# Loading the first two batches' q and k per head pair in runs of six tokens, and starting attention first, in a fused attention and multiplicative-FFN kernel

## The chip, the cores and the metric

The kernel runs on one core of a Trainium2 chip. The metric is the device time of one execution in microseconds (us), as the median of several runs. The record marks a run as ordinary or slow. PE is TensorE, DVE VectorE, ACT ScalarE, POOL GpSimd. "Span" is the length of the profiled execution, some 2 us shorter than the device time.

## The reference

Attention over 8 batches and 8 heads, 576 tokens of width 64, with 16 unmasked "beacon" keys and values in front of each sequence, then a feed-forward part without a nonlinearity, whose last two matrices are one product:

```python
scores = scale * np.matmul(q, concat([beacon_k, k]).T)       # causal over the tokens, beacons visible to all
a = exp(scores - max); a /= a.sum(-1)
attn = np.matmul(a, concat([beacon_v, v]))                   # [B=8, H=8, S=576, D=64]
x = attn.transpose(0, 2, 1, 3).reshape(4608, 512)
out = ((x @ w1) * (x @ w2) @ w3) @ w_out                     # w1, w2 512x1024, w3 1024x1024, w_out 1024x512
```

## The kernel before

All matmuls are fp16. Scores are made transposed, so each batch needs q and k as qT, kT: a head pair's 128 dimensions on the partitions, tokens in order along the free axis. From batch 2 on a DMA transposes them (30 transfers into qT and 30 into kT in the trace, 7.3 and 7.5 us in the median from issue to landing). Batches 0 and 1 are transposed on PE from token tiles of all heads, loaded through POOL's queue, which casts fp32 to fp16 on the way (the trace counts 128 KB for a tile of 128x512, two bytes a value):

```python
def load_q(b, c):                        # load_k, load_v alike; runs of 64 fp32 values per token and head
    nc.gpsimd.dma_start(
        q16s[b % NB2][:rows, c, :].rearrange("s (h d) -> s h d", h=H),
        q[b, :, ds(c * P, rows), :].rearrange("h s d -> s h d"))

def pe_transpose_qk(b, c):
    pt = psM.tile([P, 2, NT, P], FP16, name="pm")
    for j, d16 in enumerate((q16s[i], k16s[i])):
        for t in range(NT):
            nc.tensor.transpose(pt[:, j, t, :], d16[:, c, ts(t, P)], ident)
    nc.vector.tensor_copy(qTs[i][:, :, ts(c, P)], pt[:, 0])      # dense: 128 tokens in a row
    nc.scalar.copy(kTs[i][:, :, ts(c, P)], pt[:, 1])
```

Nothing of batch 0 can start until all five tiles are there. w3 and w_out come through the other queue as fp32, are cast on ACT and DVE (`cast`), and multiplied into one matrix (`fuse`, 64 matmuls) while the core waits. The FFN is a generator, `emit_ff(n)`, that puts n of its matmuls between the attention's steps. A head pair takes two steps:

```python
emit_ff(16)
for c in range(NJT):
    pe_transpose_qk(0, c)
    ...
for s in range(NS):                      # 8 steps per batch, two per head pair
    ...                                  # s == 7: rest of fuse, x transposes, batch 1's tiles
    scores(s + 1); exps(s + 1, 0)        # PE, ACT
    values(s)                            # PE, then reciprocal and scaling on DVE
    k1 = min(8, fill[s]); emit_ff(k1)
    exps(s + 1, 1); mask(s + 1, 0)       # ACT, DVE
    emit_ff(fill[s] - k1); mask(s + 1, 1)
```

In the traces each engine keeps its own instructions in program order: in e5 DVE waited 5.42 us to start a cast at 46.07 us, and a copy behind it, whose transposes PE had finished at 43.2 us, started only at 47.35.

The softmax here doesn't subtract the row's maximum and nothing guards it: scores larger than these inputs give would overflow.

## Time and profile before

| | before |
|---|---|
| time, median of 3 runs (range) | 324.86 us (323.39 to 327.02) |
| span of the profiled run | 324.5 us |
| PE busy | 286.7 us, 88% of the span |
| first exponential starts | 36.7 us |
| last values of batch 0 end | 53.1 us |
| first scores of batch 1 start | 69.2 us |
| batch 2 reached | 93.5 us |
| from there to the end | 231.0 us |

"Batch 2 reached" means the start of the second block of scores of batch 2's first head pair, throughout; from there on the two kernels have the same instructions. Columns: from:to, length, then busy us (instructions) of PE, PEld, DVE, ACT, POOL, granted clock, DMA share, GB/s.

```profile
36.70:53.10 16.40, 11.84 (x219) 7.32 (x219) 8.67 (x28) 13.34 (x18) 12.27 (x16) 1.00 1.93 170
...
69.20:93.50 24.30, 19.45 (x277) 10.98 (x278) 13.31 (x36) 16.87 (x23) 11.53 (x15) 1.00 1.57 129
```

Batch 0's attention with its filler takes 16.4 us once it has started, 4.1 us per head pair, and ACT is its busiest engine.

```profile
44.27 0.90 PE L382 MATMUL pv<-va,pT 128*128 128x65 f16 x24
```

### The profile page before, as it was taken

To read this page: it belongs to the slowest core of one execution; us is meant where nothing else is said; L and a number is where in the kernel's file an instruction comes from. 1 tells how busy PE (TensorE), PEld (TensorE's weight loads), DVE (VectorE), ACT (ScalarE), POOL (GpSimd) and SP (SyncE) were. 2 spreads that over 40 slices of the span, in tenths; PEclk is the share of its full clock that TensorE was granted. 3 is DMA by queue.
4 is the path that set the end of the run, shared out by engine and by line. 5 is a ranking of instruction groups with operands and counts; after the bars stand their busy time and mean duration, and the time that the engine had idled before them with its cause. 6 is when DMAs were issued, how large, how long until landed. Compare 5 with 4: busy or idle time off the path is not lost.

```text
span 324.5 us, 6919 instructions
## 1 busy us (share of the span) xinstructions
PE 286.7 (88%) x2776; PEld 148.2 (46%) x2776; DVE 161.5 (50%) x375; ACT 163.9 (51%) x229; POOL 117.2 (36%) x153
## 2 busy tenths in 40 slices
PE   1179777987999999999999999799999989999995
PEld 0135445543455445444554455354445544444442
DVE  3324454453664655555654655465555653343342
ACT  2325785467656665655466557464764452230320
POOL 8029869975178019505820960230000000000000
PEclk9997999999999999999999999999999999999999
DMA  8999999999999979999999999996551132202103
GB/s 242 342 288 126 167 175 146 138 144 145 119 113 187 140 86 155 208 138 126 180 176 162 138 206 175 95 146 178 68 84 65 67 32 61 111 2 91 38 2 129
DMA packets 172384, 43.72 MB, mean 135 GB/s; under 512 B 161600, under 2 KB 165696, under 8 KB 172352
## 3 DMA queue, kind: packets, MB, share of 16 engines
q0 software_dynamic: 119040, 16.52, 78.5%
q1 hardware_dynamic: 53312, 26.75, 41.7%
q8 instruction: 22, 0.36, 0.5%
q14 instruction: 10, 0.08, 0.1%
HBM read 39.32 MB, written 9.44 MB: 150 GB/s over the span
## 4 chain that ended last, share of the span: by engine, by line
PE 69%; DMA 12%; ACT 6%; DVE 5%; issue 3%; POOL 3%; DVEq 0%; ACTq 0%; POOLq 0%
PE pm L277 31%; PE pm L298 17%; PE pv L382 10%; PE ps L344 6%; DMA k<-in_beacon_k_dram 6%; ACT pT L353 5%; DMA k<-in_k_dram 3%; PE pm L255 3%; DMA qT<-q 3%; PE pm L210 1%; DVE pT L365 1%; DVE gT L290 1%; DVE x L391 1%; POOL q L101 1%; ACT a_sb L288 1%
## 5 line engine op out<-in xcount | busy, mean ns | idle before, releaser
L277 PE MATMUL pm<-xT,w 128*128 128x512 f16 x576 | 132.8, 379 | 0.6 <-ACT xT L224 0.5
L353 ACT ACTIVATE pT<-ps 128x736 f16<-128x736 f32 (+3 forms) x128 | 105.8, 863 | 35.3 <-PE ps L344 34.5
L288 ACT ACTIVATE a_sb<-pm 128x512 f32<-128x512 f32 x72 | 43.0, 597 | 81.2 <-PE pm L277 80.3
L277 PEld LDWEIGHTS <-w 128*128 128x128 f16 x576 | 53.6, 98 | 58.7 <-issue 0.9
L290 DVE TENSOR_TENSOR gT<-pm,a_sb 128x512 f16<-128x512 f32 x72 | 49.7, 690 | 47.2 <-PE pm L277 43.4
L298 PE MATMUL pm<-Wt,gT 128*128 128x512 f16 x288 | 66.7, 379 | 0.0
L110 POOL DMA_DIRECT2D va<-in_v_dram x40 | 34.0, 871 | 69.2 <-PE pv L382 68.1
L344 PE MATMUL ps<-qT,kT 64*128 64x80 f16 (+3 forms) x704 | 38.3, 228 | 13.0 <-ACT pT L353 9.8
L382 PE MATMUL pv<-va,pT 128*128 128x65 f16 x960 | 41.0, 194 | 3.4 <-DVE pT L365 2.4
L344 PEld LDWEIGHTS <-kT 64*128 64x128 f16 x704 | 20.9, 94 | 42.9 <-issue 41.2
L298 PEld LDWEIGHTS <-gT 128*128 128x128 f16 x288 | 26.9, 98 | 29.6 <-DVE gT L290 0.2
L110 POOL DMA_DIRECT2D k<-in_k_dram x40 | 34.8, 871 | 15.1 <-DMA q<-in_q_dram 10.7
L390 DVE RECIPROCAL rd<-pv 128x4 f32<-128x4 f32 x64 | 12.1, 189 | 55.0 <-PE pv L382 54.9
L101 POOL DMA_DIRECT2D q<-in_q_dram x40 | 35.5, 888 | 10.3 <-DMA k<-in_beacon_k_dram 6.1
L382 PEld LDWEIGHTS <-pT 128*128 128x128 f16 x960 | 33.0, 97 | 13.4 <-DVE pT L365 7.6
L308 DVE TENSOR_SCALAR ot<-pm 128x512 f32<-128x512 f32 x36 | 24.8, 689 | 20.9 <-PE pm L298 20.7
L391 DVE TENSOR_TENSOR x<-pv,rd 128x256 f16<-128x256 f32 x64 | 31.4, 491 | 2.4
L365 DVE TENSOR_TENSOR pT<-pT,MB 128x512 f16<-128x512 f16 x64 | 19.3, 324 | 6.4 <-ACT pT L353 6.4
L255 PE MATMUL pm<-wo,wT 128*128 128x512 f16 x64 | 18.3, 420 | 0.0
L232 PE MATMUL pm<-ident,w3c 128*128 128x128 f16 x64 | 5.8, 243 | 13.6 <-DVE w3c L152 8.3
L365 DVE TENSOR_TENSOR pT<-pT,MA 128x480 f16<-128x480 f16 x32 | 12.7, 398 | 1.8 <-ACT pT L353 1.8
L232 PEld LDWEIGHTS <-w3c 128*128 128x128 f16 x64 | 4.6, 110 | 14.1 <-DVE w3c L152 8.6
(38 smaller groups left out, 82.8 us busy)
## 6 DMA issues: line engine op xcount, KB each, us to landing
out_dram<-ot SPq DMA_DIRECT2D x36, 256.0 KB, 2.4
st<-in_moe_w_dram SPq DMA_DIRECT2D x8, 512.0 KB, 6.7
q<-in_q_dram POOLq DMA_DIRECT2D x32, 128.0 KB, 8.7
k<-in_k_dram POOLq DMA_DIRECT2D x24, 128.0 KB, 9.6
va<-in_v_dram POOLq DMA_DIRECT2D x24, 128.0 KB, 5.5
st<-in_moe_w_out_dram SPq DMA_DIRECT2D x4, 512.0 KB, 7.7
w<-in_moe_w_dram POOLq DMA_DIRECT2D x8, 256.0 KB, 7.9
k<-in_k_dram POOLq DMA_DIRECT2D x8, 112.0 KB, 7.8
```

What stands on the lines that cost most here:

```text
L101: nc.gpsimd.dma_start(q16s[b % NB2][:rows, c, :].rearrange("s (h d) -> s h d", h=H), q[b, :, ds(c * P, rows), :].rearrange("h s d -> s h d"),)
L110: nc.gpsimd.dma_start(dst[ds(p0, rows)], src[b, :, ds(s0, rows), :].rearrange("h s d -> s h d"))
L255: nc.tensor.matmul(pm, wT[:, rt, :], wo16[:, rt, :], start=(rt == 0), stop=(rt == NFT - 1),)
L277: nc.tensor.matmul(pm, w12[:, kt, ds(i * DF + kf * P, P)], xT[:, kt, ds(mc * 512, 512)], start=(kt == 0), stop=(kt == NKT - 1),)
L288: nc.scalar.activation(a_sb, pm, AF.Copy, scale=GS)
L290: nc.vector.tensor_tensor(gT[:, kf, :], pm, a_sb, ALU.mult)
L298: nc.tensor.matmul(pm, gT[:, kf, ts(mt, P)], Wt[:, kf, :], start=(kf == 0), stop=(kf == NFT - 1),)
L344: nc.tensor.matmul(ps[:, hh, ds(col, n)], kT[ds(hh * 64, 64), t, ts(jt, P)], qT[ds(hh * 64, 64), t, ds(q0, n)],)
L353: nc.scalar.activation(pT[:, :, ds(GO[g], GW[g])], pss[s][j][:, :, 0 : GW[g]], AF.Exp, scale=scale)
L365: nc.vector.tensor_tensor(blk, blk, m.unsqueeze(1).to_broadcast([P, 2, n]), ALU.mult)
L382: nc.tensor.matmul(pv[:, 2 * n + hh, 0:65], pT[:, hh, ds(col, P)], va[:, jt, 2 * t + hh, 0:65], start=(jn == 0), stop=(jn == len(BLK[i]) - 1),
L391: nc.vector.tensor_tensor(x16[:, ds(tiles[0], ni), ds(t * P, P)].rearrange("p i (h d) -> p i h d", h=2), pv[:, 0 : 2 * ni, 0:64].rearrange ...
```

## The change

Its intent is to begin batch 0's attention as soon as one head pair's q and k are there, and to do the fusion of the weights afterwards, when there is something to hide it behind. For batches 0 and 1 each head pair's q and k are loaded in fp32 so that a partition holds runs of six tokens (1536 bytes each). A DVE cast turns the pair's two heads side by side, PE transposes the six token phases, and the copy out of PSUM puts the tokens back in order. The weights' staging and casts go; both weight groups come in order through POOL's casting queue. The cut is shortened, at "..." and in the list of the two copies.

```diff
-    wc = ...; stg = ...                       # staging of the weights, cast() on ACT and DVE
+    RUN = 6
+    NR = S // RUN                             # 96
+    def load_pair(b, t):
+        engine = nc.gpsimd if b else nc.sync
+        for i, src in enumerate((q, k)):
+            st = early.tile([P, 2, RUN * D], FP32, name="st")
+            engine.dma_start(st[:NR],
+                src[b, ds(2 * t, 2)].rearrange("h (p j) d -> p h (j d)", j=RUN))
+    def pe_transpose_pair(b, t):
+        for i in range(2):
+            o16 = tiny.tile([P, RUN, P], FP16, name=f"o16_{i}")
+            nc.vector.tensor_copy(
+                o16[:NR].rearrange("p j (h d) -> p h j d", h=2),
+                early_qk[b, t, i][:NR].rearrange("p h (j d) -> p h j d", j=RUN))
+        for o16, dst, off, copy in ((q.., qT, 0, vector.tensor_copy), (k.., kT, Nb, scalar.copy)):
+            pt = psM.tile([P, 1024], FP16, name="pm")
+            for j in range(RUN):
+                nc.tensor.transpose(pt[:, ds(j * NR, NR)], o16[:NR, j, :], ident[:NR, :NR])
+            ...                               # beacons
+            copy(dst[:, t, ds(off, S)].rearrange("p (i j) -> p j i", j=RUN),
+                 pt[:, 0:S].rearrange("p (j i) -> p j i", j=RUN))
...
-    n_second = 38
+    n_first = 24
     n_kept = 10
-    n_first = 96 - n_second - n_kept
+    n_second = 96 - n_first - n_kept
-    fill[0:7] = [2, 2, 2, 1, 1, 1, 1]
+    fill[6] = 8
-    emit_ff(16)
-    for c in range(NJT): pe_transpose_qk(0, c) ...
+    pe_transpose_pair(0, 0)
+    load_pair(0, 3)
     ...
         if s == NSB - 1:
             values(s)
+            emit_ff(16)
             pe_transpose_x(0)
+            emit_ff(64 + n_first - 4 - emitted)
+            pe_transpose_pair(1, 0)
+            ...
+        if b < 2 and r % 2 == 0 and r < NSB - 2:
+            pe_transpose_pair(b, r // 2 + 1)
```

## The prediction

> **What bounds the kernel now.** I read the page's slices first, then the chain that ended last, then engine-busy time by stage, then instructions in order of time around the two places where the change acts.
>
> The slices of the page say where TensorE is idle:
>
> ```profile
> PE   1179777987999999999999999799999989999995
> ...
> PEclk9997999999999999999999999999999999999999
> DMA  8999999999999979999999999996551132202103
> ```
>
> One slice is 8.1 us. From slice 10 on PE is nearly always at 9. The first ten slices hold nearly all of its idle time. The same by stage (columns: length, then busy us and instructions of PE, PEld, DVE, ACT, POOL, then clock, DMA share, GB/s):
>
> ```profile
> 0.00:35.60 35.60, 19.56 (x144) 11.75 (x144) 13.37 (x30) 12.90 (x17) 20.85 (x33) 0.95 1.40 240
> 35.60:53.00 17.40, 12.35 (x230) 7.68 (x228) 9.09 (x28) 14.12 (x19) 13.27 (x18) 1.00 1.89 171
> 53.00:78.00 25.00, 21.28 (x207) 11.78 (x204) 11.45 (x26) 13.91 (x22) 19.92 (x25) 1.00 1.98 140
> 98.00:265.00 167.00, 160.20 (x1691) 81.69 (x1689) 92.77 (x225) 98.11 (x135) 52.06 (x65) 1.00 1.31 135
> 265.00:324.50 59.50, 55.30 (x264) 25.08 (x264) 22.92 (x35) 11.94 (x20) 0.00 (x0) 1.00 0.21 62
> ```
>
> From 98 us PE loses 11 us in 226; before 35.6 us it loses 16 in 36. What ends that idle time is in the chain, by time (start, us, what):
>
> ```profile
> 3.25 19.80 DMA k<-in_beacon_k_dram
> ...
> 23.19 0.38 PE pm L210 x4
> ...
> 24.02 2.96 PE pm L255 x8
> ...
> 28.31 1.73 PE pm L255 x8
> ...
> 36.80 1.61 ACT pT L353 x2
> ```
>
> The first k tile lands 20 us after its issue, so the first exponential starts near 36.8 us. Until then PE has only the fusion of w3 with w_out to do, paced by its own weights. The reason for the late tile is in the waits of Pool: it issued eight loads and then stood still.
>
> ```profile
> POOL k L110 <- DMA q<-in_q_dram: 7.7, 1, 7.7
> POOL q L101 <- DMA k<-in_beacon_k_dram: 6.1, 1, 6.1
> ```
>
> Eight loads are in flight at most (the ninth waits for the first, the tenth for the second or third), and the weights on the other queue held the engines meanwhile.
>
> [...]
> 1. [...] after an idle gap of 2.4 us (ended at 23.19 us) eight fusion matmuls took 2.96 us, and 1.73 us when warm. [...]
> 2. [...] a cast of 128x1024 took 0.69 us, an eviction of 128x512 from PSUM 0.42 us[...]. No row of this kernel shows a strided eviction.
> 3. [...] 0.79 us for 736 elements, 1.02 for 1024 (0.82 ns an element), and the four exponentials of a head pair at 36.70 took 3.14 us together.
> 4. [...] 135 to 155 GB/s (fp16 written) in stretches of 256-byte q, k, v rows, 293 GB/s mean in the first 24 us, when 2 and 4 KB weight rows dominated.
>
> **The change, part by part.**
> *Start.* The first two loads are now q and k of one head pair, 295 KB each, in runs of 1536 bytes, on the queue where a 512 KB load issued at 0.81 us could be cast at 4.20 us. Memsets keep DVE until about 4.0 us. Then: beacon cast 0.43[...], two casts of 768 elements at 0.56, seven k transposes, the kT copies on ACT (about 0.2 + 0.65). Scores near 8.2 us, first exponential near 8.7 us, 28 us earlier than now.
>
> *Batch 0.* Except for eight fusion matmuls there is nothing beside the attention now. A pair needs on ACT 3.14 us plus kT copies 0.75 = 3.9 us; on DVE masks 1.05 (0.41+0.40+0.24), reciprocals 0.38, normalization 0.98, casts 1.12, qT eviction 0.75 = 4.3 us. Neither is the pace: program order makes a chain. After the last exponential of a pair: scores and values of 28 matmuls 1.15, reciprocal and scaling 0.65, mask 0.35, two casts 1.0, k transposes with latency 0.5, kT copies 0.75, then two exponentials 1.45: 5.85 us per pair. The first pair has less ahead of it, 5.0; the last pair has no transposes but the eight fusion matmuls with two rows of w3 transposes, 6.1. Batch 0 ends at 8.7 + 5.0 + 2 x 5.85 + 6.1 = 31.5 us, against 53.1 us now.
>
> *What was moved behind it.* The fusion stream had given 58 matmuls by then, and gives 8 now. So afterwards: 56 fusion matmuls at 0.216 = 12.1, six rows of transposes at 0.45 = 2.7, the x transposes 2.1 (54.2 to 56.3 us now), 24 feed-forward matmuls 5.2 (48 now), one pair's q, k transposes 0.7: 22.8 us. Batch 1 starts at 54.3 us; now its first scores run at 69.2 us.
>
> *Batch 1.* It takes 62 feed-forward matmuls instead of 38 (5.2 us more) and three pairs of transposes inside its steps (2.1 us), as ten tiles' transposes before it are gone. PE's own work in a pair is 3.35 (15.5 x 0.216) + 2.3 attention + 0.7 transposes = 6.4 us. The cast chain again exceeds the filler: behind the values, scaling 0.65, a gT product 0.6, mask 0.35, casts 1.0 make 2.6 us against 1.7 us of filler, so I take 7.3 us per pair for three, 6.0 for the last, 2.1 for the x transposes: 30.0 us. Now the stage takes 24.3 us (69.2 to 93.5). Batch 2 is reached at 84.3 instead of 93.5 us.
>
> *From batch 2 on* the instructions are the same: same filler per step, same 50 held back for the tail. Loads of batch 2 come no later relative to use.
>
> *Weights.* Their SBUF staging and 12 casts (about 10 us of ACT and DVE together) go; the cast is in the Pool-queue DMA. Sources before the end of w3: 2.4 MB q, k, 1.2 MB v, 6.3 MB weights, at 300 GB/s (an estimate from the 293 above) about 33 us, and row by row earlier. The fusion uses row 2 after 31.5 us and one row per 2.2 us. w12, 4.2 MB more, is in by about 47 us. So the weights are hidden, narrowly.
>
> Sum: 93.5 - 84.3 = 9.2 us off 324.9: about 316 us.
>
> **The rivals.**
> (a) [...] Batch 0 leaves PE idle for more than half of each pair, gaps near 1.9 us. For: a 2.4 us gap sufficed once. Against: between 69 and 80 us PE had gaps of 1.2 us and stayed warm. Cold, a pair's chain gets about 1.2 us longer, four pairs 5 us: 321 us.
> (b) *The casts become the bound.* If casts and strided evictions [...]are slowed[...] (one fp32 cast took 1.10 instead of 0.69 us while Pool was issuing), each pair gets 0.8 us longer, seven pairs 5 to 6 us: again 321 to 322 us.
> (c) *Weights late.* Pool now carries v, both weight groups and batch 1 in one order, eight in flight; each late w3 row stalls PE directly. For: Pool stalled 7.7 us that way. Against: large rows and less competition. It would cost 3 to 6 us: 319 to 322 us.
> (d) *Batch 1 fills better than my chain*, as now in steady state, where a step is PE-bound. Then its pairs take 6.5 us and the total is 313 us.
>
> **Range and chances.** Centre 316 us. One of (a) to (c) alone puts it at 319 to 322, all together near 328; (d) with a faster batch 0 gives 311. The range 310 to 323 should hold eight times in ten. Faster by over 2% means under 318.4 us: 0.64, since the centre is 2.4 us below and each single rival crosses it. Slower than 331.4 us needs all of (a) to (c) and more: 0.04. Within 2%: 0.32.
>
> **What would show it.** First exponential at 8 to 10 us; batch 0's last values at 30 to 34; batch 1's first scores at 53 to 57; batch 2's at 82 to 88; from there to the end 231 us as now. Casts near 0.56 us, qT evictions near 0.75. Wrong would be: transposes of q, k over 0.1 us apart throughout batch 0 (rival a), fusion transposes waiting for a weight DMA (rival c), or a lengthened tail after batch 2, for which I have no cause.

The first exponential comes to 8.7 us, batch 0 ends at 31.5, batch 1 starts at 54.3 and batch 2 at 84.3, that is 9.2 us off 324.9 or about 316 us. The casts' 0.43 us (512 elements) and 0.56 us (768) are estimates; a straight line through the two rows named there, 0.42 us for 512 and 0.69 for 1024, gives 0.42 and 0.56. The kT copy's 0.65 us agrees with ACT's 0.58 us for 128x512 in the kernel before (at 24.07 us), taken in proportion. The qT eviction's 0.75 us was an assumption that no row shows. In (a), the gap of 2.4 us was followed by half clock from 24.4 to 27.8 us in the kernel before, but one of 2.14 us, ended at 207.1, was not; that a gap's length decides is not shown. The 0.8 us per pair in (b) is about twice the 0.41 us by which the one cast was longer. That the weights held the DMA engines rests on the first 24 us of the kernel before, where their queue moved 6.29 of 7.02 MB and took 73.9% of the 16 engines' span.

## The result, and the profile after

| | before | after | predicted |
|---|---|---|---|
| time, median of 4 runs (range) | 324.12 us (322.97 to 327.02) | **339.10 us** (338.96 to 342.94) | 316.0 us |
| first exponential starts | 36.7 | 11.3 | 8.7 |
| last values of batch 0 end | 53.1 | 45.3 | 31.5 |
| first scores of batch 1 start | 69.2 | 70.2 | 54.3 |
| batch 2 reached | 93.5 | 106.2 | 84.3 |
| from there to the end | 231.0 | 234.7 | 231 |

The kernel became slower: ratio 1.048, 95% interval 1.039 to 1.057. A ratio here is the mean time of one kernel's fast runs over that of the other's in the same rounds, so it is not quite the ratio of the medians.

The last row: the profiled run of the changed kernel was its slowest (span 340.9 us; its other runs 337.1 to 338.4), so the 3.7 us it lost behind batch 2 belong mostly to that run. Of the 15.0 us by which the median grew, the 12.7 us lost before batch 2 are the larger part. The page's slices of the changed kernel (8.5 us each):

```profile
PE   1456889968799999799999899979999999999995
...
PEclk9999999978999999989999999999999999999999
```

PE works from the second slice on, so the wait for the first tile is gone, but slices 2 to 5 stand at 4, 5, 6 and 8 where the argument needed a short batch 0. By stage:

```profile
0.00:11.30 11.30, 1.77 (x21) 1.40 (x21) 6.51 (x19) 3.42 (x3) 8.49 (x17) 1.00 1.12 184
11.30:45.40 34.10, 21.77 (x272) 15.52 (x269) 19.43 (x38) 19.45 (x23) 17.27 (x27) 1.00 1.34 210
45.40:70.20 24.80, 22.34 (x162) 11.93 (x159) 11.15 (x18) 9.13 (x14) 6.64 (x10) 1.00 0.78 77
70.20:106.20 36.00, 30.00 (x339) 16.33 (x341) 23.67 (x47) 24.05 (x31) 24.70 (x31) 0.91 1.86 140
```

Batch 0 takes 34.1 us (16.4 before), and no engine is busy for even two thirds of it: a chain, as predicted, but a longer one. Batch 1 takes 36.0 us (24.3 before). One pair of batch 0, from the exponentials that start at 16.54 to those that start at 25.11, in rows of the changed kernel's timeline (start, us, engine, line, what, count, and in brackets the idle time before and what ended it):

```profile
16.54 3.46 ACT L355 ACTIVATE pT<-ps 128x768 f16<-128x768 f32 x4
...
18.86 1.50 PE L384 MATMUL pv<-va,pT 128*128 128x65 f16 x24
...
20.40 0.20 DVE L392 RECIPROCAL rd<-pv 128x6 f32<-128x6 f32 x1 [1.86 <-PE pv L384]
20.63 0.56 DVE L393 TENSOR_TENSOR x<-pv,rd 128x384 f16<-128x384 f32 x1
...
21.11 0.40 DVE L367 TENSOR_TENSOR pT<-pT,MA 128x480 f16<-128x480 f16 x1
21.42 1.02 DVE L155 CAST o<-st 96x768 f16<-96x768 f32 x2
...
22.03 1.14 PE L166 MATMUL pm<-ident,o 96*128 96x96 f16 x12 [1.66 <-DVE o L155]
22.73 2.08 DVE L172 COPY qT<-pm 128x576 f16<-128x576 f16 x1 [0.29 <-PE pm L166]
...
23.23 0.84 PE L346 MATMUL ps<-qT,kT 64*128 64x128 f16 x14
23.33 0.17 ACT L171 COPY kT<-pm 128x16 f16<-128x16 f16 x1 [3.34 <-PE pm L168]
23.40 2.08 ACT L172 COPY kT<-pm 128x576 f16<-128x576 f16 x1
...
25.11 3.45 ACT L355 ACTIVATE pT<-ps 128x768 f16<-128x768 f32 x4
```

First, the same 24 values matmuls that took 0.90 us before take 1.50. Secondly, the casts stand behind mask, scaling and reciprocal on DVE, and PE waits 1.66 us for them. Thirdly, each copy into qT and kT takes 2.08 us, of which the page has eight on each engine:

```profile
L172 DVE COPY qT<-pm 128x576 f16<-128x576 f16 x8 | 16.6, 2078 | 0.8 <-PE pm L166 0.6
L172 ACT COPY kT<-pm 128x576 f16<-128x576 f16 x8 | 16.7, 2083 | 0.0
```

Set against the prediction's sum of 5.85 us per pair (taking the middle of each group of four exponentials as the end of a pair's last exponential):

| term | predicted | measured | from to |
|---|---|---|---|
| scores and values | 1.15 | 2.1 | 18.27 to 20.36 |
| reciprocal and scaling | 0.65 | 0.83 | to 21.19 |
| mask | 0.35 | 0.32 | to 21.51 |
| casts | 1.0 | 0.93 | to 22.44 |
| k transposes with latency | 0.5 | 0.89 | to 23.33 |
| kT copies | 0.75 | 1.78 | to the next exponential, 25.11 |
| two exponentials | 1.45 | 1.73 | half of 3.45 |
| sum | 5.85 | 8.6 | |

The chain has the predicted order. Its terms are off in two ways: PE's own work at 1.6 to 1.7 times its warm duration (and the exponentials that wait for it), and the copy.

The last pair of batch 0 has no such copy ahead of it, and is too long all the same: 9.8 us from the end of the third pair's exponentials, near 35.5, to the last values at 45.3, where 6.1 was predicted. Its last exponential stands in ACT's order behind the fusion's copy out of PSUM, and ACT is idle until the eighth fusion matmul is done:

```profile
43.20 0.59 ACT L268 CAST Wt<-pm 128x512 f16<-128x512 f32 x1 [4.18 <-PE pm L259]
```

### The profile page after: what moved, and what is told of

Read it like the earlier page. It is cut to its first block, busy times and chain, and to the rows that moved or that the text cites. A ratio compares the mean times of both kernels' runs of the same rounds, so it can differ in the third digit from the quotient of the medians.

```text
span 340.9 us, 6952 instructions
## 1 busy us (share of the span) xinstructions
PE 297.5 (87%) x2800; PEld 155.1 (46%) x2800; DVE 179.3 (53%) x387; ACT 168.7 (49%) x229; POOL 113.0 (33%) x152
## 4 chain that ended last, share of the span: by engine, by line
PE 64%; DMA 11%; ACT 9%; DVE 6%; issue 4%; POOL 2%; SPq 2%; DVEq 0%; POOLq 0%
PE pm L279 26%; PE pm L300 15%; PE pv L384 9%; PE ps L346 6%; ACT pT L355 5%; DMA qT<-q 5%; PE pm L259 4%; DMA k<-in_k_dram 3%; DMA xT<-x 2%; ACT kT L172 2%; PE pm L166 2%; DVE o L155 2%; PE pm L249 1%; DMA bst<-in_beacon_k_dram 1%; DVE pT L367 1%
## 5 line engine op out<-in xcount | busy, mean ns | idle before, releaser
L279 PE MATMUL pm<-xT,w 128*128 128x512 f16 x576 | 135.3, 384 | 3.8 <-DMA xT<-x 2.5
L355 ACT ACTIVATE pT<-ps 128x736 f16<-128x736 f32 (+3 forms) x128 | 107.6, 872 | 34.8 <-PE ps L346 34.1
L346 PE MATMUL ps<-qT,kT 64*128 64x80 f16 (+3 forms) x704 | 41.5, 244 | 17.1 <-ACT pT L355 10.5
L384 PE MATMUL pv<-va,pT 128*128 128x65 f16 x960 | 43.5, 200 | 2.0 <-DVE pT L367 1.7
L384 PEld LDWEIGHTS <-pT 128*128 128x128 f16 x960 | 35.4, 101 | 12.4 <-DVE pT L367 7.1
L112 POOL DMA_DIRECT2D k<-in_k_dram x30 | 26.2, 872 | 9.5 <-DMA va<-in_v_dram 4.5
L103 POOL DMA_DIRECT2D q<-in_q_dram x30 | 26.1, 871 | 5.3 <-DMA k<-in_k_dram 4.1
L367 DVE TENSOR_TENSOR pT<-pT,MB 128x512 f16<-128x512 f16 x64 | 19.8, 327 | 13.4 <-ACT pT L355 13.4
L166 PE MATMUL pm<-ident,o 96*128 96x96 f16 x96 | 8.8, 252 | 16.1 <-DVE o L155 15.8
L172 DVE COPY qT<-pm 128x576 f16<-128x576 f16 x8 | 16.6, 2078 | 0.8 <-PE pm L166 0.6
L172 ACT COPY kT<-pm 128x576 f16<-128x576 f16 x8 | 16.7, 2083 | 0.0
L166 PEld LDWEIGHTS <-o 96*128 96x128 f16 x96 | 6.2, 120 | 19.7 <-DVE o L155 19.7
```

Of the source, the lines that this page charges most:

```text
L103: nc.gpsimd.dma_start(q16s[b % NB2][:rows, c, :].rearrange("s (h d) -> s h d", h=H), q[b, :, ds(c * P, rows), :].rearrange("h s d -> s h d"),)
L112: nc.gpsimd.dma_start(dst[ds(p0, rows)], src[b, :, ds(s0, rows), :].rearrange("h s d -> s h d"))
L172: copy(dst[:, t, ds(off, S)].rearrange("p (i j) -> p j i", j=RUN), pt[:, 0:S].rearrange("p (j i) -> p j i", j=RUN),)
L279: nc.tensor.matmul(pm, w12[:, kt, ds(i * DF + kf * P, P)], xT[:, kt, ds(mc * 512, 512)], start=(kt == 0), stop=(kt == NKT - 1),)
L346: nc.tensor.matmul(ps[:, hh, ds(col, n)], kT[ds(hh * 64, 64), t, ts(jt, P)], qT[ds(hh * 64, 64), t, ds(q0, n)],)
L355: nc.scalar.activation(pT[:, :, ds(GO[g], GW[g])], pss[s][j][:, :, 0 : GW[g]], AF.Exp, scale=scale)
```

## The experiments

Three causes stand against each other. *Strided copies*: the copies write fp16 with a step of six elements, and that costs 2.08 us instead of some 0.7. *Clock*: PE is held at half rate through batch 0, rival (a) of the prediction. *Queue of casts*: the casts come too late in DVE's order, whatever their own length. "Behind" in this section is the stretch from batch 0's last values to batch 1's first scores. The stage marks come from the profiled run of each kernel, so single ones carry an uncertainty of about a microsecond; those of the changed kernel and of e4 are from their slowest runs.

| kernel | time, us (range, runs) | ratio to before (95%) | first exp | batch 0 ends | batch 1 | batch 2 |
|---|---|---|---|---|---|---|
| before | | 1 | 36.7 | 53.1 | 69.2 | 93.5 |
| after | 339.10 (338.96–342.94, 4) | 1.048 (1.039–1.057) | 11.3 | 45.3 | 70.2 | 106.2 |
| e3, dense copies | 329.06 (327.78–331.15, 4) | 1.017 (1.012–1.022) | 9.1 | 39.3 | 62.8 | 97.1 |
| e1, stepped reads | 331.95 (330.56–333.31, 4) | 1.026 (1.021–1.032) | 9.9 | 39.7 | 63.2 | 97.3 |
| e2, PE reorders | 335.04 (333.46–336.37, 4) | 1.035 (1.030–1.039) | 9.4 | 41.1 | 65.2 | 101.7 |
| e4, e1 + dummies | 327.65 (326.29–330.06, 4) | 1.012 (1.006–1.018) | 9.5 | 37.5 | 61.0 | 94.5 |
| e5, e1 + early casts | 327.09 (325.07–328.18, 4) | 1.009 (1.004–1.014) | 9.3 | 34.5 | 63.7 | 93.1 |
| e6, e1 + batch 1 as before | 325.15 (323.63–326.53, 4) | 1.004 (0.999–1.009) | 9.3 | 39.7 | 63.9 | 93.5 |
| e7, e5 + dummies | 327.01 (325.24–328.58, 4) | 1.011 (1.005–1.017) | 8.6 | 36.7 | 62.2 | 91.6 |
| e8, e5 with one cast moved | 320.07 (318.64–321.94, 3) | 0.989 (0.982–0.995) | 9.3 | 33.4 | 55.9 | 85.4 |
| e9, e6 + early casts + dummies | 322.76 (320.83–323.18, 4) | 0.995 (0.990–1.000) | 9.8 | 35.9 | 60.2 | 89.8 |
| e10, e9 + other filler | 319.92 (318.30–321.87, 6) | 0.989 (0.984–0.994) | 9.3 | 36.2 | 57.1 | 86.7 |
| e11, e8 + other filler | **316.07** (315.63–316.92, 6) | **0.975** (0.971–0.980) | 9.7 | 35.3 | 54.5 | 84.0 |

A fourth run of e8 was slow (324.0 us) and is left out. The kernels ran in four calls: e3, e1, e2 and the probe; e4 to e7; e8 to e10; e11. The kernel before had medians of 323.49, 324.21, 323.50 and 324.03 us in them (in the last, three slow runs of eleven are left out).

### e3: the copies without their step

```diff
-            copy(dst[:, t, ds(off, S)].rearrange("p (i j) -> p j i", j=RUN),
-                 pt[:, 0:S].rearrange("p (j i) -> p j i", j=RUN))
+            copy(dst[:, t, ds(off, S)], pt[:, 0:S])
```

The tokens of batches 0 and 1 are in the wrong order. The comparison with the reference passed all the same: the scores are so small here that attention is nearly uniform.

> The changed kernel with its qT and kT evictions written densely, without the reordering (the result is wrong on purpose: tokens stay in the order of the transposes). Theory A, the step of 12 bytes on the SBUF side is the whole cost of the 2.08 us copies: they take about 0.45 us (VectorE) and 0.65 us (ScalarE), eight pairs save about 1.4 us each on the chain, 11 us in all: about 328 us. Theory B, the cold TensorE clock in batch 0 is the larger part: copies fall as much, but values of batch 0 still take 1.45 us and the time falls by less than 6 us, to over 333. Theory C, late loads set the pace: copies fall, the time stays within 3 us of 339.

Measured: 329.06 us, 10 us less than after. Batch 0's stage went from 34.0 to 30.2 us and batch 1's from 36.0 to 34.3. The rows of the copies in e3:

```profile
L172 ACT COPY kT<-pm 128x576 f16<-128x576 f16 x8 | 5.2, 644 | 0.0
...
L172 DVE COPY qT<-pm 128x576 f16<-128x576 f16 x8 | 3.6, 455 | 1.3 <-PE pm L166 1.1
```

Same data, same shape, same PSUM source: 2078 against 455 ns on DVE, 2083 against 644 on ACT. The step alone is the difference, and with all that follows from it, it is worth 9 us before batch 2. It isn't all: e3 is still slower than the kernel before, and its PE is still slow in batch 0:

```profile
23.18 1.50 PE L381 MATMUL pv<-va,pT 128*128 128x65 f16 x24
```

### p1: what a step costs

Copies of 128x576 fp16 behind the end of the changed kernel, one after the other, from PSUM to SBUF with write steps of 1, 2, 3, 4, 6, 8 and 12 elements, alternating DVE and ACT, then with the step on the reading side, then from SBUF to SBUF.

```diff
+    probe = psM.tile([P, 1024], FP16, name="pm"); ...
+    for n in (1, 2, 3, 4, 6, 8, 12):                                          # written out
+        nc.vector.tensor_copy(qT0.rearrange("p (i j) -> p j i", j=n), probe.rearrange("p (j i) -> p j i", j=n))
+        nc.scalar.copy(kT0.rearrange("p (i j) -> p j i", j=n), probe.rearrange("p (j i) -> p j i", j=n))
+    ...                                                                       # "p i j" for stepped reads
```

> The changed kernel with copies of 128x576 fp16 behind its last matmul, on VectorE and on ScalarE: PSUM to SBUF with write steps of 1, 2, 3, 4, 6, 8 and 12 elements, PSUM read with steps of 288 and 96 elements, SBUF to SBUF with steps 1, 4, 6, 8. [...] If it is any step other than 1: all about 2.1 us. If it grows with the step: a ramp. Total about 20 us over the changed kernel.

Measured in one run (370.0 us as a whole, longer by the probe; state unknown, but durations within it are compared with one another only). The DVE rows for steps 1, 2, 3, 4, 6, 8, 12 and the stepped read, in this order, from the probe's timeline:

```profile
334.41 0.45 DVE L482 COPY qT<-pm 128x576 f16<-128x576 f16 x1
...
335.56 0.80 DVE L484 COPY qT<-pm 128x576 f16<-128x576 f16 x1 [0.70 <-ACT kT L483]
...
337.22 1.11 DVE L486 COPY qT<-pm 128x576 f16<-128x576 f16 x1 [0.86 <-ACT kT L485]
...
339.52 1.43 DVE L488 COPY qT<-pm 128x576 f16<-128x576 f16 x1 [1.18 <-ACT kT L487]
...
342.44 2.06 DVE L490 COPY qT<-pm 128x576 f16<-128x576 f16 x1 [1.50 <-ACT kT L489]
...
346.64 2.70 DVE L492 COPY qT<-pm 128x576 f16<-128x576 f16 x1 [2.13 <-ACT kT L491]
...
352.11 2.68 DVE L494 COPY qT<-pm 128x576 f16<-128x576 f16 x1 [2.77 <-ACT kT L493]
...
357.52 0.76 DVE L496 COPY qT<-pm 128x576 f16<-128x576 f16 x1 [2.74 <-ACT kT L495]
```

ACT took 0.64, 0.80, 1.11, 1.43, 2.06, 2.70, 2.68 and, for the stepped read, 0.64 us. So two engines with different speeds in the dense case (0.45 and 0.64 us) cost the same from step 2 on (0.80 on both): what is paid is not the engine's dense rate but the step of the write. From there the time rises by 0.31 to 0.32 us per element of step and stops rising at 8: of the outcomes named beforehand the ramp came, with an end. Step 4 takes 1.43 us, three times the dense 0.45 on DVE, and step 2 takes 0.80. All six times lie within 0.03 us of a fixed 0.17 us plus 0.316 us per element of step, counted up to 8, an estimate from these rows. Why the rise ends at 8 is not shown. A stepped *read* of PSUM costs ACT nothing (0.64 us in both cases) and DVE 0.3 us (0.76 against 0.45). Copies from SBUF to SBUF at steps 1, 4, 6, 8 took 0.30, 0.81, 1.13, 1.45 us on DVE and 0.68, 1.47, 2.10, 2.73 on ACT: DVE pays about half there. Why is open.

### e1: the step moved to the reading side

```diff
-                dst[:, t, ds(off, S)].rearrange("p (i j) -> p j i", j=RUN),
-                pt[:, 0:S].rearrange("p (j i) -> p j i", j=RUN),
+                dst[:, t, ds(off, S)].rearrange("p (i j) -> p i j", j=RUN),
+                pt[:, 0:S].rearrange("p (j i) -> p i j", j=RUN),
```

Same result, same instructions, another order of elements: the write is dense, the read of PSUM jumps by 96 elements.

> The changed kernel with the reordering on the read side: PSUM read with a step of 192 bytes, SBUF written densely; result right. If the cost lies in the SBUF write alone: copies about 0.7 us, total about 329 us. If a step on the PSUM side costs as much: copies stay near 2 us and the total near 339 us.

Measured: 331.95 us, correct; copies 758 ns on DVE and 644 on ACT, which is what the prediction had assumed (0.75, 0.65). Two swapped letters give back 7 of the 15 us; about 329 us had been expected for this case. The rest has other causes.

### e2: PE does the reordering

```diff
+            for u in range(2):                        # halves of 288 tokens, fp32 in PSUM; shortened
+                h0, hn = u * (NR // 2), NR // 2
+                pt = psM.tile([P, 512], FP32, name="pm")
+                for j in range(RUN):
+                    nc.tensor.matmul(pt[:, 0:hn*RUN].rearrange("p (i j) -> p j i", j=RUN)[:, j, :],
+                                     o16[:NR, j, :], ident[:NR, ds(h0, hn)])
+                ...                                   # beacons
+                copy(dst[:, t, ds(off + h0 * RUN, hn * RUN)], pt[:, 0 : hn * RUN])
```

> The changed kernel with the reordering done by TensorE: it multiplies by the identity into fp32 PSUM with a step of 24 bytes, in two halves, and the evictions are dense in and out; result right. If only the SBUF write with a step is slow: two evictions of 288 of about 0.42 us each per tensor, total 329 to 331 us. If TensorE's writes with a step are slow, its 12 matmuls of 48 columns take well over 0.1 us each and the total is over 334 us.

Measured: 335.04 us, between e1 and after, and over the 334 us that had been named as the sign of slow stepped writes. The copies are dense and fast, 451 and 405 ns for 288 elements, but there are twice as many, and 192 matmuls of 258 ns in place of 96. That a single one takes as long as before (mean 252 ns in the changed kernel) hides what the step costs, as it has 48 columns now and had 96. By the trace's single records their starts stand 43 ns apart at full clock and 80 ns at half, just as far as those of the 96-column transposes in the changed kernel, so a column that PE writes with a step takes twice as long. Neither the fp32 output nor the weight loads explain it: in the same run the fusion's matmuls write 512 fp32 columns every 216 ns, and the values matmuls, each with its own weights, start 29 ns apart. Of the three ways to put the tokens in order it is the second best.

### e4: dummy matmuls to keep the clock up

```diff
+    def warm(n):
+        pt = psM.tile([P, 512], FP32, name="pm")
+        for _ in range(n): nc.tensor.matmul(pt[:, 0:256], MB[:, 0:128], MB)
+    warm(19)                                  # while the first loads are on their way
     pe_transpose_pair(0, 0)
     ...
+        if b == 0 and r % 2 == 0 and r < NSB - 2:
+            warm(12)                          # before a pair's transposes
```

> The read-side reordering kernel (332 us) with dummy matmuls on TensorE that nobody reads: 19 of 256 columns before the first transposes, 12 before each pair's transposes in batch 0, where TensorE waits for casts anyway. Theory B, the halved clock lengthens batch 0 by 1.2 us a pair: 24 values matmuls take 0.9 instead of 1.5 us, the period of a pair falls from 7.2 to about 6 us, the total to 327 us or a little less. Rival, the chain through VectorE and ScalarE alone sets the period: clock full, total within 1.5 us of 332.

Measured: 327.65 us, 4 us below e1 by median, with batch 2 2.8 us earlier. The values are at the old speed at the same place of batch 0:

```profile
21.33 3.15 ACT L360 ACTIVATE pT<-ps 128x768 f16<-128x768 f32 x4
...
23.27 0.90 PE L389 MATMUL pv<-va,pT 128*128 128x65 f16 x24
...
27.67 3.97 ACT L360 ACTIVATE pT<-ps 128x768 f16<-128x768 f32 x5
```

So rival (a) did happen. Net of the dummies it is worth 4 us by the medians and 3 by the marks. The pair between the exponentials at 21.33 and 27.67 took 6.34 us (7.46 in e1); 5.85 was predicted. With dense copies and a warm PE the predicted chain is right within half a microsecond. The column of the granted clock would not have told: it stands at 1.00 in the changed kernel's batch 0, where the matmuls take 1.6 times as long, because that view counts the time before the first recorded change as full. The durations show it (the pair's transposes start 80 ns apart there, as they do at 72.3 us where the recorded clock is 0.5, and 43 ns apart at full clock), and so do the times of the changes, which the packed trace holds. The first change, to full clock, comes at 41.5 us in the changed kernel, 35.2 in e1, 24.7 in e5, 18.7 in e8 and 25.3 in e11, and at 17.5 in the kernel before, long before its batch 0 starts. Nor did the dummies of e4 hold the clock throughout: after 6.2 us it was at full, but from 9.6 to 13.0 and from 16.4 to 19.8 at half again.

### e5, e8: casts one step earlier

The casts of pair t+1 move from the step of its transposes to the step before, behind less urgent work:

```diff
+        if b < 2 and r % 2 == 1 and r < NSB - 4:
+            cast_pair(b, (r + 1) // 2 + 1)    # was inside pe_transpose_pair, one step later
```

For batch 1's first pair, e5 casts right behind the x transposes; e8 casts eight FFN matmuls before its transposes:

```diff
             pe_transpose_x(0)
-            cast_pair(1, 0)                   # e5
-            load_pair(1, 3)
-            emit_ff(64 + n_first - 4 - emitted)
+            emit_ff(64 + n_first - 12 - emitted)
+            cast_pair(1, 0)                   # e8
+            load_pair(1, 3)
+            emit_ff(8)
             pe_transpose_pair(1, 0)
```

> The read-side reordering kernel (332 us) with each pair's casts issued one step earlier, into the time in which VectorE waits for the values matmuls; nothing else moved. Theory D, the casts behind scaling and mask hold the transposes up in every pair: TensorE's waits of 1.6 us for the casts vanish, six pairs gain 1.0 to 1.5 us each, total 323 to 326 us. Rival, the wait moves on to the kT copies and exponentials: total over 329 us.

Measured for e5: 327.09 us, between the two forecasts. Batch 0 is 4.6 us shorter than in e1 (25.2 against 29.8), but "behind" is 29.2 us against 23.5, because a cast was put in front of a load that had not landed, and DVE's order made the fusion wait with it:

```profile
46.07 0.42 DVE L151 CAST b<-bst 16x512 f16<-16x512 f32 x1 [5.42 <-DMA bst<-in_beacon_k_dram]
...
47.35 1.27 DVE L257 COPY wT<-pm 128x1024 f16<-128x1024 f16 x2
```

The transposed weights' copy that PE needed stood behind it; PE idled 4.91 us, and right after it the clock fell to half for 3.4 us (48.6 to 52.0). e8 undoes this alone.

> The early-cast kernel mended: its first cast of batch 1 now stands eight fusion-stream matmuls before its transposes instead of right behind the x transposes, where VectorE stood 5.4 us for a beacon load. If that stall is why early casts gave 5 us back: 321 to 323 us, the fusion stage without a wait of TensorE on wT. If it is not: still 326 to 328 us.

Measured for e8: 320.07 us, ratio 0.989: the first version below the kernel before, if by less than 2%. No fusion matmul behind batch 0 waits for wT any more. By stage:

```profile
9.60:33.40 23.80, 16.17 (x268) 12.07 (x267) 13.32 (x35) 14.78 (x23) 12.16 (x19) 1.00 1.35 206
33.40:55.90 22.50, 22.10 (x164) 12.17 (x163) 9.87 (x18) 7.68 (x14) 11.60 (x17) 1.00 1.37 189
55.90:85.40 29.50, 26.76 (x340) 15.25 (x341) 20.65 (x48) 19.86 (x31) 22.73 (x29) 1.00 2.13 151
```

Against e1, batch 2 comes 11.9 us earlier, and PE's clock came with it without a dummy. Rows of e8's timeline:

```profile
15.28 0.92 PE L352 MATMUL ps<-qT,kT 64*128 64x128 f16 x8
...
16.12 1.68 PE L390 MATMUL pv<-va,pT 128*128 128x65 f16 x24
...
17.61 1.15 PE L172 MATMUL pm<-ident,o 96*128 96x96 f16 x12
...
18.81 0.52 PE L352 MATMUL ps<-qT,kT 64*128 64x128 f16 x14
...
19.51 3.15 ACT L361 ACTIVATE pT<-ps 128x768 f16<-128x768 f32 x4
...
22.19 0.68 PE L172 MATMUL pm<-ident,o 96*128 96x96 f16 x12
...
23.61 3.96 ACT L361 ACTIVATE pT<-ps 128x768 f16<-128x768 f32 x5
```

The next pair's casts now begin at 21.26 us, ahead of reciprocal, scaling and mask, and no transpose of batch 0 waits for them; from 15.0 to 19.6 us PE works without a pause, and 14 scores take 0.52 us at 18.81, against 0.84 in the changed kernel. (Just before, PE had waited 0.68 and 2.40 us for v; the work that piled up may be why it then ran without a pause.) A pair, 19.51 to 23.61, takes 4.1 us, the pace of the kernel before. How much of the 11.9 us is the cast and how much the clock it brought along cannot be split as a whole, but for one pair it can. The same pair, from one group of four exponentials to the next, stands in e1 and e5 at half clock (their first change to full, at 35.2 and 24.7 us, comes after it or at its end) and in e4 and e8 at full:

| | half clock | full clock |
|---|---|---|
| casts late | 7.46 us (e1) | 6.34 us (e4) |
| casts early | 5.37 us (e5) | 4.10 us (e8) |

Early casts take 2.1 to 2.2 us off the pair in either state, full clock 1.1 to 1.3 us with either casts: here the two add. (The dummies of e4 end at 25.49 us in this pair, and its transposes start with the cast at 25.84, so they are not in its chain.) The rows of e1, then of e5:

```profile
21.13 3.28 ACT L355 ACTIVATE pT<-ps 128x768 f16<-128x768 f32 x4
...
28.59 3.28 ACT L355 ACTIVATE pT<-ps 128x768 f16<-128x768 f32 x4
```

```profile
19.30 3.28 ACT L361 ACTIVATE pT<-ps 128x768 f16<-128x768 f32 x4
...
24.67 3.96 ACT L361 ACTIVATE pT<-ps 128x768 f16<-128x768 f32 x5
```

### e6, e9, e10: batch 1 as before

e6 takes e1 and loads and transposes batch 1 in token tiles, as the kernel before does.

```diff
-            emit_ff(64 + n_first - 4 - emitted)
-            pe_transpose_pair(1, 0)
+            emit_ff(64 - emitted)
+            for c in range(NJT):
+                emit_ff((n_first - 4) // NJT)
+                pe_transpose_qk(1, c)
     ...                                       # its loads by tile as well
-        if b < 2 and r % 2 == 0 and r < NSB - 2:
+        if b < 1 and r % 2 == 0 and r < NSB - 2:
             pe_transpose_pair(b, r // 2 + 1)
```

> The read-side reordering kernel (332 us) with batch 1's q and k loaded and transposed in tiles of tokens as in the kernel before, batch 0 by pairs. Batch 1's stage of 34 us loses its casts and pair copies (about 3 us a pair for three pairs of wait and work), the stage ahead of it gains ten tiles of transposes, 4 us: total 326 to 329 us if the pair scheme costs most in batch 1; within 1.5 us of 332 if it costs the same in either place.

Measured: 325.15 us, 7 us below e1, no different from the kernel before. With late casts, pairs in batch 1 are worse than tiles: the stage takes 29.6 us here and 34.1 in e1, at nearly the same "behind" (24.2 against 23.5). In e1 the clock is at half for 3.4 us of this stage (65.9 to 69.3), here never. e9 adds the early casts to it for batch 0, dummies, and the v loads ahead of POOL's mask building:

```diff
+    for c in range(NJT): load_v(0, c)         # moved before the affine_selects of MA, MB
+    warm(38)                                  # 128 columns each
+    cast_pair(0, 0)
     ...
+        if s in (0, 2): warm(8)
```

> Batch 0 by pairs with the read-side reordering, early casts, a warm clock (dummy matmuls at the start and in two steps), v loads issued ahead of the mask selects; batch 1 in tiles as in the kernel before. From the parts: 325 less 4 for the clock and 5 for the casts: 316 to 319 us, so faster than the kernel before by about 2%. If the parts hide one another: 321 to 323 us.

Measured: 322.76 us, batch 2 at 89.8 us, later than e8 with its pairs in both batches (85.4). The warm clock that it was to have failed to come: the page shows it down to half in batch 0, by the trace from 8.9 to 25.9 us, so this run doesn't test that part.

```profile
PEclk9558999999999999999999999999999999999998
```

e10 changes only the filler of batch 0:

```diff
-    fill[6] = 8
+    fill[4:7] = [4, 8, 8]
-        k1 = min(8, fill[s])
+        k1 = min(8, fill[s]) if b else 0      # the fusion's matmuls behind the second exponential
```

> The same with 20 instead of 8 fusion matmuls inside batch 0, put behind the exponentials of their step, so that ScalarE does not wait for them: two to four us less than the combined kernel without it, 313 to 316 us. If batch 0 is held by TensorE once warm: no change against the combined kernel.

Measured: 319.92 us, 2.8 us below e9 as expected, though not the 313 to 316 us that were built on e9's forecast. The clock was at half here too, from 9.1 to 12.5 and from 16.0 to 26.2 us. The reason for the edit lies in e8's timeline, where, as in the changed kernel, the fusion's copy on ACT stands in front of an exponential and waits for the eighth fusion matmul:

```profile
31.27 0.59 ACT L274 CAST Wt<-pm 128x512 f16<-128x512 f32 x1 [3.70 <-PE pm L265]
```

### e7: early casts and dummies together

```diff
+    warm(19)                                  # e5 + the dummies of e4, 8 instead of 12
+            warm(8)
```

> Early casts and dummy matmuls together (19 at first, 8 before each pair's transposes in batch 0). If the halved clock and the cast chain add up: 319 to 321 us, under the kernel before. If one hides behind the other: no better than the better of the two alone.

Measured: 327.01 us, the same as e5. Batch 2 came 1.5 us earlier in the profiled run, but the median didn't move. That does not show that the two effects cannot add (in the table of the pair above they do). The dummies are in the chain when the casts are not: the eight in this row stand in front of transposes whose casts had ended at 23.06 us. And they did not hold the clock, which was at half from 15.5 to 19.0 and from 22.4 to 25.8 us.

```profile
23.43 1.90 PE L254 MATMUL pm<-MB 128*128 128x256 f16 x8
```

The stall of e5 in "behind" is in both (4.9 us in e5, 2.9 here).

### e11: e8 with the filler and the v loads of e10, without dummies

```diff
+    for c in range(NJT): load_v(0, c)         # before the affine_selects, as in e9
-    fill[6] = 8
+    fill[4:7] = [4, 8, 8]
-        k1 = min(8, fill[s])
+        k1 = min(8, fill[s]) if b else 0
```

> The mended early-cast kernel (321 us) without any dummy work, with 20 instead of 8 fusion matmuls inside batch 0 behind the exponentials of their steps, and v loads ahead of the mask selects. ScalarE no longer waits 2 to 4 us for the fusion in step 6, and 2 to 3 us of fusion move into batch 0's gaps: 316 to 319 us, over 1.5% faster than the kernel before. If the gap that filled is lost again to the clock or to the v loads: 320 to 322 us, as without it.

Measured: 316.07 us in six runs, 2.5% below the kernel before; correct. By the marks batch 0 holds more of the fusion now, so it takes longer than in e8 (25.6 us against 24.1), and "behind" gets shorter by more (19.1 against 22.5); batch 1 is the same (29.5). PE's clock is not mended: it is at half until 25.3 us, longer than in e8. A wait is left at the start of batch 0, for v, which the faster chain reached before it had landed (with a second of 0.41 us; in e8 they were 0.68 and 2.40):

```profile
15.83 0.54 PE L390 MATMUL pv<-va,pT 128*128 128x65 f16 x7 [1.29 <-DMA va<-in_v_dram]
```

## Why the prediction was wrong

It said 316 us with a range of 310 to 323, and 339.1 was measured. By its own steps:

- *Start, first exponential 8.7.* Measured 11.3; e3 and e1, with fast copies, 9.1 and 9.9. The number was right but for the copy, in part by luck: DVE began its casts at 6.09 us, after a wait of 1.83 us for the beacons, and not at 4.0 when the memsets end, but the prediction's terms before the scores left over a microsecond to spare.
- *Batch 0, 22.8 us by a chain of 5.85 us per pair.* **This is the step that failed.** 34.0 measured: against the prediction's parts, 1.8 us more in the first pair, 2.7 and 2.9 in the next two, 3.7 in the last. The idea, a chain in program order rather than a bound engine, was right, and so was its order; casts, mask and scaling are within 0.2 us. Three terms were mis-sized. "kT copies 0.75" measured 1.78 on the path (2.08 for the main copy alone), and on DVE the qT eviction "0.75" measured 2.08. The terms on PE were taken at full clock, though rival (a) had been seen: scores, values and transposes together 1.65 predicted, 3.0 measured. The sum was 8.6 instead of 5.85. e3 and e1 showed the copy's part, e4 the clock's; with both put right e4 has 6.34. The third is the last pair, "6.1": 9.8 measured, 9.7 in e1, so the copy is not it, and still 8.4 in e4 and e8 at full clock. The prediction counted the eight fusion matmuls and two rows of transposes, but not that ACT's copy of their result stands before the last exponential and waits 4.18 us for the eighth (3.70 in e8); e10 and e11 put the matmuls behind the exponentials.
- *The moved work, 22.8 us.* 24.9 measured, 23.5 in e1, 22.5 in e8. Right.
- *Batch 1, 30.0 us.* 36.0 measured. 34.1 with fast copies (e1), 29.5 with early casts (e8). So the copy explains at most 1.9 us here, and the chain itself was underestimated by about 4. The clock has a part in it: it was at half for 6.8 us of this stage in the changed kernel (72.2 to 79.0) and for 3.4 in e1, and never in e8 or e6, which can have cost at most half of that time directly. e6 (29.6) and e8 show that the 4 us go with the late casts, the clock's share included.
- *From batch 2 on, 231.* Right: 230 to 232 in the experiments' profiles but for e4's, 231.0 before. The changed kernel's profiled run had 234.7; its other runs, shorter by 2.5 to 3.8 us, speak for that run rather than the kernel. Its trace shows what it was: PE waited 2.49 us for a transposed x at 143.22, and the clock then fell to half for 3.4 us (143.9 to 147.3). The probe p1, the same program up to its end, waited 1.92 us there, kept its clock, and needed 229.2 us from batch 2 to its last scaled output, where this run needed 231.7. e4's 233.6 has such a spell too (211.0 to 214.4).
- *Rival (a), the clock.* It occurred, at about its predicted size: "about 1.2 us longer" per pair, and the PE terms above are 1.3 us longer. In batch 1, where the prediction did not look for it, it occurred as well. It was treated as an alternative and given too little weight; that PE would work in short pieces was known from the sum itself, though that this sets the clock is not shown (last section).
- *Rival (b), casts and strided evictions.* It named the strided copy, and allowed 0.8 us a pair for casts and evictions. The measured copy is 3.6 ns per element (2078 ns over 576), nearly three times the 0.75 us assumed for it. Most casts kept their 0.53 to 0.55 us. Single casts of the changed kernel took 0.79, 0.81 and 0.92 us, each while Pool was issuing a DMA; but those at 7.16 and 71.70 us, beside such an issue too, took 0.54 and 0.55, so that the issue is the cause is not shown.
- *Rival (c), late weights.* Did not happen in the changed kernel: no transpose or matmul of the fusion waits for a weight's DMA there. A first trace of it, a wait of 0.78 us, is in e11, where the chain is faster.
- *Rival (d).* Did not happen with late casts.

All three of the prediction's adverse effects "together near 328" was the worst case given. The true size was beyond it because the bound on the copy was made without a measurement of a stepped write (2.06 us at step 6 in p1, 0.45 dense on DVE), and because the last pair of batch 0 and batch 1's chain were too short in the sum besides. A row for a strided eviction did not exist in the profile before, and the prediction said so; it then put a figure there all the same, without widening the range.

That e11 ends at the predicted 316 us is no confirmation: it gets there with casts off the chain, other filler, and v loaded earlier, none of which the prediction had.

## What to carry to other kernels

If a copy out of PSUM has to permute, put the step on the copy's read of PSUM and write SBUF densely: with 576 fp16 values per partition it is 0.64 to 0.76 against 2.08 us here, and nothing else changes. Do not leave it to PE, whose stepped writes took twice as long per column (43 ns for 48 columns, as long as for 96 without a step). When work is brought forward into a stretch where engines wait for each other, every instruction counts by its place in each engine's order, so do casts and loads one step ahead of their use, but never ahead of data that has not landed, and keep the copy of a filler's result behind the instruction that the chain needs next. Judge TensorE's clock by the durations of like matmuls (24 of the values took 0.90 or 1.50 us where the column of the clock read 1.00 both times), and size a kind of access that no row of the profile shows with a wide range, or not at all.

## What the traces show of the clock

Between two recorded changes the clock stays in one state for a whole number of stretches of 3.41 us: in the changed kernel 30.72, 6.83, 64.85, 3.41 and 194.56 us (9, 2, 19, 1 and 57 of them), in the kernel before 6.83, 3.41 and 296.96 (2, 1 and 87). The length of PE's stretches of work fits less simply. In batch 0 of the changed kernel none reached 3 us before 36 us, and PE stayed slow until 41.5; in e8 it sped up after 3.8 us without a pause (15.0 to 18.8). But e1 sped up at 35.2 with no stretch over 2.8 us, and e11 did not after 4.3 us with pauses of 0.1 us at most (9.2 to 13.5). What sets the change is not shown.
